# A new order for all engines of a delta-rule and gated-MLP kernel, operations and buffers as before

## The chip, the cores and the metric

One core of a Trainium2 chip runs the whole program. The metric is device time in microseconds, the median of several executions. PE is the matrix engine (TensorE), DVE VectorE, ACT ScalarE, POOL GpSimd, and SP issues the loads and stores. Each engine executes its own list of instructions in order, and waits on semaphores for what the others have to deliver.

## The reference

Four batches of eight heads run a delta rule over 768 time steps with a 48 x 48 state per head; its output, 384 wide, goes through a gated MLP with a mixing over time.

```
k_n = k / (norm(k) + 1e-6)
for t in range(768):
    y[t]  = q[t] @ state
    v_old = k_n[t] @ state
    state = state + beta[t] * outer(k_n[t], v[t] - v_old)
h = relu(x @ w_in);  u, v = h[:, :512], h[:, 512:]
v_n = (v - mean(v)) / sqrt(var(v) + 1e-6)
out = (u * (w_spatial @ v_n + b_spatial)) @ w_out
```

w_in and w_out come as 64-bit floats, all else as 32-bit.

## The kernel before, in words

The recurrence is cut into chunks of 64 time steps. Two batches are worked on at a time, so there are 24 steps s (two rounds of 12); within a round each needs the state of the one before.

**Preparation.** Steps come in six groups g of four. For a group, PE makes the products of the keys (kk blocks, line 492), copies bring them to SBUF (L500, L503), DVE transposes the diagonal parts (L525), a chain of small instructions makes the norms and scales (L533 to L543), and then a triangular inverse is built column by column. Group 0 does it for blocks of 16 (L576 and L581, 15 columns), with ACT's L549 writing the diagonal first, L586 copying the result out, DVE's L595 transposing it back, and two rounds of widening (two PE blocks w16e and w16f, ACT's L683 between them, DVE's L685 and shifts behind them). The other groups do it for blocks of 32: 61 "lane" instructions on DVE (L563 and L568) beside their counterparts on POOL, then L595 and shifts on ACT and POOL (L327, zeros L331 and L333). For each pair of steps L625, PE blocks e and f, ACT's L646 and L651 widen the result to 64.

**A step.** PE blocks kq (masked by DVE's L724), a (subtracted from v by L747), qs, b (copied by ACT's L777), c (added to the state by L792 or L790) and pu; the output goes out by ACT's L807, is put in place by small loads (xs), and is cast and split by L827 and L828. v is scaled before by L707. The loads of step s + 2 take the buffer of step s.

**Weights.** w_in and w_out are made 32-bit by hand (load, L392, L394 to L397, L398, L400 to L403), and all weights are split in a high and a low half for the faster matmuls (L383 on ACT, L384 on DVE or POOL).

**MLP.** Chunks of two or three large matmuls (B512, B256, B384) with their evictions: L851 to L880 for v and its norm, L904 for u, L945, L962 to L968 for the gate, L983 for the output.

All of this is 2642 operations in a plan. `ORDER` lists them in the order in which the program issues them; each engine's own list is what the order leaves for it. A number w in it stands for operation w // 4, and w % 4 chooses among the engines on which that operation may run (DVE or POOL for the subtractions, ACT or POOL for some copies).

```
    words = [int(w) for w in ORDER.split()]
    with tc.manual_schedule():
        P.issue([divmod(w, 4) for w in words])
```

Buffers and PSUM banks are taken from small pools when an operation is issued, in the order of the list, so the list also says which unit each operation gets.

Of the kernel before, what the change touches and what calls it, by code (L numbers as in the profile page):

```python
# [36 lines left out]
28 0 24 52 64 40 928 448 8 32 20 12 56 37 4 68 61 44 936 1076 72 85 80 48  # L37
89 1064 92 97 292 100 344 108 452 112 456 116 1080 120 468 124 128 132 1100 1084 136 140 500 460
76 1068 144 608 464 396 296 148 552 1072 1088 472 152 1692 932 104 348 476 312 504 156 480 164 1696
352 485 168 1104 172 300 176 624 612 180 184 304 489 188 192 628 196 200 356 400 204 616 632 416  # L40
208 696 621 212 492 216 1108 220 160 224 508 1092 228 692 232 664 497 404 236 2384 240 1096 244 2348
248 308 1129 252 2336 256 512 1112 1121 260 264 408 268 1729 272 276 520 556 280 316 412 668 680 284
1125 672 684 677 360 940 944 560 364 708 688 1732 572 368 712 716 948 564 1117 952 1736 516 420 372
320 376 16 324 380 568 720 956 724 524 1004 728 328 968 576 732 988 332 980 740 736 1000 985 960
1008 972 289 744 1012 424 748 528 580 428 752 584 432 994 965 1060 1016 996 976 437 1640 1020 532 1132
1644 1048 1029 1026 1689 1040 1648 756 1652 588 1136 1656 1660 1054 1140 1044 1144 1056 1148 1664 536 1668 1152 1034
1680 1700 1156 1672 1160 1036 1980 2340 1704 1164 1676 1168 592 1708 1189 1684 336 540 760 1724 2344 1712 1172 1180
1740 1176 1184 596 1716 1196 1296 1200 1308 1744 1312 1984 1720 764 1204 341 636 1208 1748 1992 1212 440 1216 1220
1752 1988 1224 2029 1996 1228 1232 1756 385 1236 1760 1240 1244 1248 1768 388 601 1252 1256 1260 1772 1764 1324 1796
2032 1328 1264 1340 1784 392 652 640 2000 2332 444 1788 2040 1268 1344 2008 2036 1792 1356 2004 1360 644 1272 1780  # L50
2020 2048 1372 2044 1800 2016 1376 1276 2052 656 648 1776 2056 1280 700 661 2060 1284 1804 2068 1288 1292 2072 704
1808 872 2012 2352 2076 544 2024 1300 1388 2372 2356 1304 1392 2360 1316 1404 1320 1408 2084 2064 549 1332 2092 1336
892 1348 604 1916 2081 1352 2088 1420 1364 2100 2096 1424 1368 1436 2104 1380 1440 1384 1452 1396 1836 876 2108 1400
1456 880 1192 1412 1468 2112 1416 1472 2120 1428 1432 1484 1920 1444 2124 1488 1448 1924 884 1500 1460 2152 1928 1464
1504 1932 888 1476 2144 1516 2376 1480 1520 1492 2132 896 1936 2380 3796 1496 1532 1508 1940 2364 1536 1512 1944 900
1840 1524 1548 3784 904 1528 1552 1540 1844 2140 2368 1544 1564 1556 1812 1568 2400 2136 1560 1580 1572 1816 1576 1584
2116 2148 1588 1848 909 2396 1592 2128 1852 1856 2961 2392 1948 2388 2964 912 1620 1952 2404 1601 1628 2972 1609 1626
1956 1960 1596 1606 1964 2968 1632 1968 1614 1820 1636 3013 916 1616 2912 1824 2408 2452 1828 920 2916 2156 2412 2976
768 3016 2920 2416 2160 2924 1832 2928 2932 3020 1972 2164 1861 2940 2420 2936 2424 2168 2428 1864 2952 2432 2980 3432
# [1046 lines left out]
```

## Time and profile before

| | us |
|---|---|
| median of 3 runs | 452.54 (451.09 to 455.63) |
| the profiled execution | 450.03 |
| its span, first to last instruction | 448.3 |
| PE busy / DVE / ACT / POOL | 401.3 / 284.8 / 252.6 / 173.9 |

The profiled execution is one of its own, a little faster than the median. Its span leaves out 1.73 us around the program. Durations in the prediction are those of this one execution.

### The profile page before, as it was taken

Reading aid. Unit: us, or ns where it says so; the run is one execution under the profiler, and the core shown is the slowest. Engines: PE = TensorE matmul, PEld = TensorE weight load, DVE = VectorE, ACT = ScalarE, POOL = GpSimd, SP = SyncE. Lnnn points to the kernel's source line nnn. Section 1 sums busy time; section 2 is a strip of 40 time slices with the busy share of each in tenths; the row PEclk is TensorE's granted clock in tenths of the full one; section 3 lists DMA queues with packets and bytes.
Section 4 is the critical chain, followed back from the end, with each engine's and each line's share of the span. In section 5 each row is a group of like instructions: output and inputs, shape, how many; then the busy total and the mean of one; then the engine's idle time right before and its main releaser. Section 6 shows DMA issues by size and latency. Waiting matters only on the chain.

```text
span 448.3 us, 19504 instructions
## 1 busy us (share of the span) xinstructions
PE 401.3 (90%) x8648; PEld 363.5 (81%) x8648; DVE 284.8 (64%) x697; ACT 252.6 (56%) x551; POOL 173.9 (39%) x343
## 2 busy tenths in 40 slices
PE   4325677999899999999999999999999999999996
PEld 3214566778688898778889889899889899999996
DVE  3799899988868876638898988833313324431331
ACT  3898763796677742976466834373426772231112
POOL 5270278628770863313785465612111110110010
PEclk9555586999999999999999999999999999999999
DMA  8941057222542332122351232032300000000102
GB/s 269 350 161 40 4 185 263 95 86 93 194 140 102 117 123 102 41 95 95 108 178 39 85 112 83 5 111 86 111 30 1 2 35 1 1 35 37 54 35 89
DMA packets 16020, 42.51 MB, mean 95 GB/s; under 512 B 3392, under 2 KB 7616, under 8 KB 15936
## 3 DMA queue, kind: packets, MB, share of 16 engines
q1 hardware_dynamic: 15936, 41.27, 27.1%
q8 instruction: 68, 1.11, 1.0%
q14 instruction: 16, 0.13, 0.1%
HBM read 35.36 MB, written 4.72 MB: 89 GB/s over the span
## 4 chain that ended last, share of the span: by engine, by line
PE 76%; DMA 8%; ACT 5%; DVE 5%; SPq 2%; issue 2%; POOL 1%; ACTq 0%; DVEq 0%; POOLq 0%
PE ps L453 76%; DMA bn<-in_bun 3%; SPq L348 2%; DMA ke<-in_k_t 2%; DMA vf<-in_w_in 2%; ACT xt L327 1%; DVE xt L595 1%; DVE ps L581 1%; DVE prod L576 1%; DMA xs<-xs 1%; DMA bn<-in_k_t 1%; ACT xh L827 1%; ACT tn L646 1%; DVE wsp_l L384 0%; DVE pt L724 0%
## 5 line engine op out<-in xcount | busy, mean ns | idle before, releaser
L453 PE MATMUL ps<-wsp_h,vf 128*128 128x256 f32 x480 | 104.3, 286 | 0.0
L453 PEld LDWEIGHTS ps<-wsp_h,vf 128*128 128x128 f32 x480 | 80.8, 188 | 1.4
L453 PE MATMUL ps<-wsp_l,vf 128*128 128x256 f32 x240 | 67.5, 281 | 0.0
L568 DVE TENSOR_TENSOR ps<-ps,prod 128x60 f32<-128x60 f32 (+9 forms) x150 | 46.0, 307 | 4.3
L563 DVE TENSOR_TENSOR prod<-ps,la 128x60 f32<-128x60 f32 (+9 forms) x150 | 44.7, 298 | 4.0
L453 PEld LDWEIGHTS ps<-wsp_l,vf 128*128 128x128 f32 x240 | 45.2, 188 | 0.3
L962 DVE TENSOR_TENSOR gt<-ps,bbc 128x512 f32<-128x512 f32 x18 | 12.4, 692 | 43.6 <-PE ps L453 43.6
L568 POOL TENSOR_TENSOR wl<-wl,prod 128x36 f32<-128x36 f32 (+4 forms) x90 | 31.9, 354 | 6.7
L563 POOL TENSOR_TENSOR prod<-wl,la 128x36 f32<-128x36 f32 (+4 forms) x90 | 31.1, 345 | 5.9
L453 PE MATMUL ps<-ke 64*64 64x64 f32 x704 | 18.2, 253 | 13.8 <-ACT xt L327 5.2
L453 PE MATMUL ps<-wout_h,g 128*128 128x384 f32 x112 | 30.5, 342 | 0.0
L453 PEld LDWEIGHTS ps<-ke 64*64 64x64 f32 x704 | 15.2, 161 | 17.4 <-ACT xt L327 7.0
L983 ACT COPY ob<-ps 128x384 f32<-128x384 f32 x24 | 11.4, 479 | 26.9 <-PE ps L453 23.2
L453 PE MATMUL ps<-bn 64*64 64x64 f32 x832 | 20.1, 241 | 6.6 <-DMA bn<-in_k_t 3.6
L777 ACT COPY w<-ps 128x384 f32<-128x384 f32 x24 | 11.5, 480 | 24.6 <-PE ps L453 24.5
L968 POOL TENSOR_TENSOR xt<-gt,xt 128x512 fp32r<-128x512 f32 x3 | 3.9, 1285 | 55.1 <-ACT xt L967 55.1
L453 PE MATMUL ps<-wsp_h,bn 128*128 128x256 f32 x96 | 24.7, 281 | 0.0
L453 PEld LDWEIGHTS ps<-bn 64*64 64x64 f32 x832 | 16.6, 150 | 9.9 <-issue 3.9
L651 ACT COPY xt<-ps 32x256 f32<-32x256 f32 x48 | 17.4, 363 | 10.2 <-PE ps L453 9.5
L453 PE MATMUL ps<-xh,win_h 128*128 128x256 f32 x120 | 22.5, 296 | 0.8 <-ACT vr L851 0.8
L807 ACT COPY xs<-ps 112x512 f32<-112x512 f32 x22 | 12.9, 585 | 17.4 <-PE ps L453 17.2
L453 PE MATMUL ps<-wout_h,xt 128*128 128x384 f32 x80 | 22.0, 338 | 0.0
(192 smaller groups left out, 1088.8 us busy)
## 6 DMA issues: line engine op xcount, KB each, us to landing
bn<-in_bun SPq DMA_DIRECT2D x22, 896.0 KB, 4.9
ke<-in_k_t SPq DMA_DIRECT2D x22, 256.0 KB, 3.7
out<-ob SPq DMA_DIRECT2D x24, 192.0 KB, 1.9
vf<-in_w_in SPq DMA_DIRECT2D x6, 512.0 KB, 6.9
g<-in_w_sp SPq DMA_DIRECT2D x3, 768.0 KB, 4.4
g<-in_w_out SPq DMA_DIRECT2D x4, 384.0 KB, 3.1
bn<-in_bun SPq DMA_DIRECT2D x2, 640.0 KB, 8.1
xs<-xs SPq DMA_DIRECT2D x66, 16.0 KB, 2.4
```

The costliest lines, as they stand in the source:

```text
L327: (nc.scalar.copy if e == "ACT" else ENG[e].tensor_copy)(out=out_, in_=in_)
L348: return P.add({"SP": 0.55}, lambda: nc.sync.dma_start(out=out_() if callable(out_) else out_, in_=in_() if callable(in_) else in_), rd, w ...
L453: nc.tensor.matmul(o, l, r, start=start, stop=stop)
L563: P.add({eng: cost}, lambda: e.tensor_tensor(out=dst if j == i0 else pt, in0=w[:, :n, j : j + 1].broadcast_to([128, n, m]), in1=la3[:, j, ...
L568: P.add({eng: cost}, lambda: e.tensor_tensor(out=dst, in0=dst, in1=pt, op=ALU.add), rd=[pk], wr=[key], due=due)
L576: P.add({"DVE": cost}, lambda: nc.vector.tensor_tensor(out=dst if j == 0 else pt, in0=w4[:, :, :n, j : j + 1].broadcast_to([128, 2, n, m]) ...
L581: P.add({"DVE": cost}, lambda: nc.vector.tensor_tensor(out=dst, in0=dst, in1=pt, op=ALU.add), rd=[("prod", "DVE")], wr=["wp"], due=due)
L651: P.add({"ACT": 0.46}, lambda r=i(a), f=f: nc.scalar.copy(out=v()[r, :, f, :], in_=pq4[r, :, f - 1, :]), rd=["pe0"], wr=[("fo", s + par, a ...
L777: P.add({"ACT": 0.48}, lambda: nc.scalar.copy(out=v3(w, 192), in_=v3(pc, 512)[:, :, 0:192]), rd=["pc"], wr=[("w", s % 2)], due=due + 2)
L807: nc.scalar.copy(out=x.rearrange("p (s j t) -> p s j t", s=4, j=2)[0:KR, :, :, s % 2 * 64 : s % 2 * 64 + 64], in_=pq.rearrange("p (s c) -> ...
L962: P.add({"DVE": 0.69}, lambda: nc.vector.tensor_tensor(out=gt(), in0=v3(bank(h.unit), 256), in1=v3(sums(p, half), 256) if p else bias(th), ...
L983: P.add({"ACT": 0.48}, lambda: nc.scalar.copy(out=ob_[t.unit], in_=bank(h.unit)[:, :DM]), rd=[("po", b, th, o)], wr=[("ob", b, th, o)], du ...
```

## The change

Only the list changes. Another search wrote it, one that judges an order by draws of noise on the durations that change during the search. The operations, their dependencies and the pools are the same. By engine, the list before has 886 operations on PE, 697 on DVE, 502 on ACT, 321 on POOL and 164 on SP; the new one 886, 691, 496, 333 and 164. 140 operations run on another engine than before (98 between DVE and POOL, 34 between ACT and POOL, 8 between ACT and DVE). Within its engine's list an operation moves by a median of two places on PE, DVE and POOL, four on ACT, one on SP; at most by 60.

```diff
 ORDER = """
-28 0 24 52 64 40 928 448 8 32 20 12 56 37 4 68 61 44 936 1076 72 85 80 48
-89 1064 92 97 292 100 344 108 452 112 456 116 1080 120 468 124 128 132 1100 1084 136 140 500 460
-76 1068 144 608 464 396 296 148 552 1072 1088 472 152 1692 932 104 348 476 312 504 156 480 164 1696
-352 485 168 1104 172 300 176 624 612 180 184 304 489 188 192 628 196 200 356 400 204 616 632 416
+8 0 28 20 12 52 64 40 16 80 4 448 32 24 56 36 68 1064 60 44 936 88 1076 73
+85 292 49 928 96 93 104 100 452 108 1080 152 112 116 456 120 124 1100 1084 128 160 500 132 460
+296 1068 344 136 464 140 608 148 1088 1072 144 552 156 468 1692 1112 164 472 300 396 168 312 1696 932
+172 1104 176 476 180 480 504 184 2348 348 1108 188 485 508 192 612 624 196 352 200 204 1092 628 489
...
 10336 10340
 """
```

The parts of it that the prediction speaks of, by engine (operation number and line):

```
DVE ahead of the first L576, behind the first L543
  before  74 L392, 37 L543, 118 L398, 87 L392, 119 L400, 126 L392, 41 L576
  after   36 L543, 41 L576   (118, 119, 126, 87 stand between the next L576 and L581)
DVE between the last L581 of group 0 and L595
  before  139 L392, 79 L398, 71 L595
  after   432 L707, 71 L595   (432 was on POOL; 158 L384 is on POOL now)
ACT between L586 and the first L683
  before  103 L396, 168 L383, 171 L383, 90 L396, 140 L394, 91 L397, 143 L397
  after   128 L395, 281 L327, 102 L395, 90 L396, 77 L396, 168 L383, 171 L383, 140 L394, 103 L396
SP, the first loads
  before  7, 13, 16, 10 keys, 232 step 0, 112 w_in, 269 keys, 20 beta, 266 keys, 73, 86 w_in, 275 keys, 125 w_in, 152 w_sp, 99, 138 w_in
  after   7, 13, 16, 10 keys, 20 beta, 112 w_in, 266, 269 keys, 73 w_in, 232 step 0, 275 keys, 125, 86 w_in, 152 w_sp, 272 keys, 138 w_in
DVE behind the first lane of group 1 (299 L563)
  before  300 L563, 436 L747, 191 L384, 301 L568
  after   83 L403, 300 L563, 301 L568, 191 L384, 96 L403, 302 L563, 436 L747
PE, steps 0 to 2
  before  425 b, 585 kk, 427 c, 435 a, 429 pu, 496 e, 437 qs, 438 b, 440 c, 442 pu, 508 kq, 500 f, 510 a
  after   425 b, 427 c, 585 kk, 435 a, 429 pu, 496 e, 437 qs, 438 b, 442 pu, 440 c, 500 f, 508 kq, 510 a
```

## Rows read from the trace of the kernel before

**Rows 1.** The page: busy time of each engine with its share of the span, and the granted clock of PE in 40 slices of 11.2 us, in tenths of full speed.

```profile
PE 401.3 (90%) x8648; PEld 363.5 (81%) x8648; DVE 284.8 (64%) x697; ACT 252.6 (56%) x551; POOL 173.9 (39%) x343
...
PEclk9555586999999999999999999999999999999999
```

**Rows 2.** Busy time by stretch (from and to in us, then the length; x is the number of instructions; then the clock as a share of full speed, the DMA share and GB/s).

```profile
0.00:20.00 20.00, 7.15 (x226) 6.21 (x227) 10.19 (x24) 11.35 (x20) 8.42 (x31) 0.79 0.88 297
20.00:45.00 25.00, 9.38 (x558) 8.31 (x561) 23.55 (x57) 22.73 (x40) 10.21 (x12) 0.50 0.37 130
...
60.00:93.42 33.42, 26.76 (x707) 21.83 (x699) 30.95 (x78) 20.90 (x41) 25.77 (x47) 0.85 0.50 170
93.42:200.00 106.58, 102.69 (x2795) 87.96 (x2795) 79.90 (x224) 73.72 (x176) 51.52 (x118) 1.00 0.33 109
200.00:448.30 248.30, 244.13 (x3957) 228.93 (x3947) 127.25 (x290) 112.83 (x249) 73.23 (x129) 1.00 0.18 60
```

The five busy times in each row are PE, its weight loads, DVE, ACT and POOL.

**Rows 3.** The chain of work that ended last, in order of time: start, length, what.

```profile
11.97 6.82 DMA vf<-in_w_in
...
42.37 0.39 ACT ob L683
...
327.59 117.20 PE ps L453 x899
444.86 0.48 ACT ob L983
```

**Rows 4.** DVE in order of time, up to L595 of group 0: start, length, line, operation, out<-in, shapes; in brackets the idle time before it and what ended that.

```profile
13.57 0.27 DVE L506 MEMSET ps<- 128x256 f32 x1
...
18.81 0.43 DVE L392 TENSOR_SCALAR ut<-vf 128x512 uint32<-128x512 uint32 x1 [2.17 <-DMA vf<-in_w_in]
...
22.85 0.95 DVE L384 TENSOR_TENSOR wsp_l<-g,wsp_h 128x768 fp32r<-128x768 f32 x1
...
28.92 0.85 DVE L392 TENSOR_SCALAR ut<-vf 128x512 uint32<-128x512 uint32 x1
29.70 0.68 DVE L398 SCALAR_TENSOR_TENSOR ut<-vf,ut 128x512 uint32<-128x512 uint32 x1
30.30 2.07 DVE L595 STREAM_TRANSPOSE xt<-wl 128x1024 f32<-128x1024 f32 x1
```

**Rows 5.** ACT in order of time, around the first L683.

```profile
29.05 0.59 ACT L586 COPY wl<-ps 128x512 f32<-128x512 f32 x1 [0.44 <-DVE ps L581]
...
30.16 1.55 ACT L383 CAST wsp_h<-g 128x768 fp32r<-128x768 f32 x2
...
33.98 0.37 ACT L683 ACTIVATE ob<-ps 128x256 f32<-128x256 f32 x1
```

**Rows 6.** PE in order of time: the first block w16e, and the first matmuls of block e of steps 0 and 1 and of steps 4 and 5.

```profile
32.42 1.26 PE L453 MATMUL ps<-xt,bbc 32*16 32x16 f32 x128 [6.85 <-DVE xt L595]
...
47.05 0.63 PE L453 MATMUL ps<-tn,xt 32*32 32x32 f32 x27 [1.15 <-DVE tn L625]
...
93.42 0.75 PE L453 MATMUL ps<-tn,xt 32*32 32x32 f32 x64
```

**Rows 7.** Busy time by stretch, as in rows 2: from the end of L586 to L683; from L525 of group 1 to its first lane; the lanes, up to L595; from L595 to L625.

```profile
29.64:33.98 4.34, 1.56 (x140) 1.52 (x144) 4.31 (x5) 4.34 (x8) 2.80 (x3) 0.50 0.26 92
...
46.91:57.10 10.19, 7.45 (x236) 6.82 (x240) 8.96 (x20) 7.97 (x21) 1.56 (x3) 0.50 0.10 18
57.10:86.68 29.58, 23.77 (x765) 20.08 (x758) 27.83 (x78) 16.66 (x33) 24.00 (x46) 0.79 0.52 182
...
86.68:92.65 5.97, 5.19 (x88) 4.23 (x88) 5.13 (x5) 5.62 (x11) 3.27 (x6) 1.00 0.53 184
```

**Rows 8.** DVE in order of time, beside the lanes of group 1 and after them.

```profile
57.94 1.51 DVE L384 TENSOR_TENSOR wout_l<-g,wout_h 128x384 fp32r<-128x384 f32 x1
...
65.21 1.28 DVE L384 TENSOR_TENSOR win_l<-ut,win_h 128x512 fp32r<-128x512 f32 x2
...
68.38 2.05 DVE L384 TENSOR_TENSOR wsp_l<-g,wsp_h 128x768 fp32r<-128x768 f32 x1
...
85.97 0.54 DVE L790 TENSOR_TENSOR s<-s,ps 112x384 f32<-112x384 f32 x1
...
93.28 0.52 DVE L384 TENSOR_TENSOR wout_l<-g,wout_h 128x384 fp32r<-128x384 f32 x1
...
94.53 0.96 DVE L828 TENSOR_TENSOR xl<-xs,xh 128x768 fp32r<-128x768 f32 x1
```

**Rows 9.** POOL in order of time, two of the same splits.

```profile
57.76 1.27 POOL L384 TENSOR_TENSOR win_l<-ut,win_h 128x512 fp32r<-128x512 f32 x1
...
67.81 1.81 POOL L384 TENSOR_TENSOR wsp_l<-g,wsp_h 128x768 fp32r<-128x768 f32 x1 [0.28 <-ACT wsp_h L383]
```

**Rows 10.** Groups of instructions by line, engine and shape: busy time, mean ns of one, idle time before them and what ended it.

```profile
L965 DVE TENSOR_TENSOR gt<-gt,ut 128x512 f32<-128x512 f32 x15 | 10.8, 720 | 0.5
...
L707 DVE TENSOR_TENSOR bn<-bn,nn 128x384 f32<-128x384 f32 x7 | 4.3, 611 | 1.9 <-DMA bn<-in_bun 1.9
...
L403 DVE TENSOR_TENSOR ut<-ut 128x512 f32<-128x512 f32 x3 | 2.0, 685 | 0.0
...
L965 POOL TENSOR_TENSOR gt<-gt,ut 128x512 f32<-128x512 f32 x9 | 12.1, 1341 | 12.9 <-DVE gt L962 6.5 <-DVE st L868 6.2
```

212 rows, old and new, of the table ORDER are left out of this document.

## The prediction, made before the change was run

> **What bounds the kernel now.** I read the shares and slices of the page first. PE is busy 90% of the span, and the granted clock stands at half in slices 2 to 5, comes back in slice 6 and dips once more in slice 7 (67 to 78 us) before it stays [rows 1]. So there are two stages with different limits, and the table of stretches puts numbers on them [rows 2]. In the first 45 us PE works 16.5 us and DVE 33.7 us, of which 23.55 in the 25 us from 20 to 45. From 60 to 93.42 DVE is still the fuller one (30.95 of 33.42 us, PE 26.76). From 93.42 to 200 PE is busy 102.69 of 106.58 us, from 200 to the end 244.13 of 248.30. 93.42 is where PE starts block e of steps 4 and 5 [rows 6], the first PE work that needs group 1 of the preparation.
>
> The reading for this change: the PE list is a fixed heap of matmuls. Before and after, exactly the same 66 PE operations stand ahead of that block e, and 820 from it on, so an order can only win by bringing that point forward, or by closing PE gaps behind it. The gaps behind it are 3.89 + 4.17 us [rows 2], and 3.5 us of the latter are the last copy and store, from 444.8 [rows 3] to 448.3, which no order removes: 4.6 us are on offer there. What sets 93.42 is the chain of group 0, in the chain view a file of DVE and ACT instructions from the first loads on [rows 3], and then the 61 lane instructions of group 1 on DVE.
>
> **The change, part by part.** I wrote the two lists out by engine, and took every duration from the trace of before. The profiled execution took 450.03 us: 448.3 of span and 1.73 around it. The median of the runs shown is 452.54, so I work against 450.03 and carry the difference over to 452.54. About 1% of that, 4.5 us, is the least that a measurement of this kernel can tell from no change.
>
> *The wait for a weight load goes.* In the old list DVE has L392 of op 126 ahead of the first L576. It waits 2.17 us for a w_in load that was issued at 11.97 and lands at 18.79 [rows 3, 4], with nothing to do meanwhile. The new list has the first L576 straight after the two L543, and puts the L392s between later lane instructions. There, adding up the durations, op 126 comes at about 18.5, and its load is issued with 0.5 MB less ahead of it, so I cost that edit's new wait at nothing; should the load be as late as before, it is 0.3 us. L549, on which the first L576 also depends, moves ahead of two L397 on ACT. DVE also has less work ahead of L595: L506 (0.27), one L384 (0.95), one L392 (0.85) and one L398 (0.68) go behind it or to POOL [rows 4], one L707 (0.61 [rows 10]) comes from POOL: -2.1 us. L595 moves from 30.30 by 2.2 (the wait alone) to 4.3 us (both in full). Some of it is lost to L549 and to the copy L586 (0.59 [rows 5]), so I take -3.5.
>
> *ACT takes most of that back.* L595 releases block w16e on PE, and its result is copied by L683 on ACT. Between L586 and L683 ACT has 7 instructions in the old list and has no gap (4.34 us busy of 4.34 [rows 7]); in the new list it has 9. Two more, at 4.34 us for 7, are +1.2; and two of the nine are the casts of the second w_sp load, which is issued once the first is split, on POOL as far as I can see at about the old time: they stood at 30.16 [rows 5] and are 6th and 7th in line now, so that they can hardly come much earlier, and L683, which follows two instructions behind them, lands at some 32.4. It was already at ACT's pace: its input ended at 33.68 [rows 6], it began at 33.98 [rows 5]. So it comes 1.6 us earlier and not 3.5; by ACT's two instructions alone it would be 2.3. Now w16f, L685, the shifts, again w16e and w16f and L625 follow. DVE has 1.3 us more between L595 and L685, hidden by PE's w16f; ACT 0.5 less up to its first shift; from there to L625 the DVE work is the same within 0.1 us. So block e of steps 0 and 1 (47.05 [rows 6]) and L525 of group 1 (46.91) come some 1.4 us earlier.
>
> *From L525 to the lanes of group 1.* DVE has 8.96 us busy in these 10.19 us [rows 7]; the new list puts 0.6 us more there (one L402 and one L403 in, one L403 and one memset out), which its 1.23 us of idle may or may not cover, since one part of that idle is the wait for PE's block c of step 0. The start of the lanes moves by -1.4 to -0.2; I take -0.8.
>
> *The lanes.* From 57.10 to 86.68 DVE executes 78 instructions with 27.83 us busy of 29.58 [rows 7]: this is the bound, and work in or out counts whole. Out go an L384 of w_sp (2.05), an L384 of w_in (half of the 1.28 for two) and an L790 (0.54), in come two L403 (0.69 each) and one L384 of w_in (0.64) [rows 8, 10]: -1.2 us. But the 2.05 us ran beside POOL's L384 of the same size (1.81 at 67.81 [rows 9]); L828, a subtraction of the same size and types, takes 0.96 alone [rows 8], and by that the sum is -0.1. I take the middle, -0.6. POOL gets one L384 of w_sp and one of w_in there and gives up one of w_in and one L403, some 0.7 us more; it has 5.6 us of idle in this stretch [rows 7], so its own lanes stay hidden.
>
> A split on DVE is stretched by one on POOL: L384 of w_out takes 1.51 us at 57.94, after POOL's L384 began at 57.76, and 0.52 us at 93.28 [rows 8, 9]. The Trainium skill, page "SBUF — State Buffer", section "Who interferes with whom", has a rule for that: a DVE instruction with two SBUF inputs and a GpSimd instruction that reads SBUF block each other in full. By the rule each of the three instructions that come to DVE would also meet a POOL lane, and the sum for the lanes would be above zero; by the rows of DVE alone it is -0.6.
>
> *From L595 to block e of steps 4 and 5.* One L384 (0.52), the L790 (0.54 [rows 8]) and one L747 come between L595 and L625, an L403 and an L724 go: one instruction more, +0.4, against 0.84 us of idle in that stretch [rows 7]. I take +0.3.
>
> *Sum up to block e:* -0.8 - 0.6 + 0.3 = -1.1 us, between -2.6 and +0.1.
>
> *Behind block e.* All PE blocks and chunks are there in both lists, moved by a median of two places. The trace cannot show what the gaps of another interleaving are. From below, the 4.6 us on offer go entirely; from above, I let as much be added. I take 0, nearest to the fact that the number of changes between small and large matmuls is about the same (80 and 83 in the two lists), as is the cover: for links of one instruction between two PE blocks (L646, L777, L747, L503, L724, L807 and so on) I counted the PE work that the list puts between both blocks against the duration of the link, and what is short sums to 14.3 us in the old list and to 14.0 in the new. Other parts (swaps of DVE and POOL in the gate's L965 and L968, order of loads, the last operations of the list) stand under full PE slices and cost nothing; if that cover fails, a swap costs 0.6 us, the difference of L965 on the two engines [rows 10].
>
> So 450.03 - 1.1 = 448.9 against the profiled execution, and 452.54 - 1.1 = **451.4** against the median.
>
> **The rivals.**
> *A, the early gain is kept.* If ACT executes its nine instructions sooner than I think (the w_sp load landing early), all of L595's 3.5 us reaches block e. For it: the chain view has L683 only in its second round [rows 3]. Against it: ACT without a gap. Time 449.0, still inside 1%.
> *B, faster: the PE gaps close as well.* A search that judges orders by disturbed durations might leave more room between the links. Sum -1.1 - 4.6 = -5.7, time 446.8. For it: 8 us of gaps, most of them ahead of 200 us. Against it: the cover counted above is the same.
> *C, slower: step 1 is held up on DVE.* L747 of step 1 has five more instructions ahead of it (L403 twice, L384 and two short lane instructions: 0.69 + 0.69 + 1.51 is 2.9 us, and the lanes some more [rows 8, 10]). Behind it stand block b of step 1, its state and its outputs, and all of steps 2 and 3, which PE has in line ahead of block e. The clock came back to full in slice 6 and was at half again in slice 7 [rows 1]; a PE that waits at 59 may keep the half clock for longer. Three us of delay and two more of slower matmuls: +5.0, time 457.5. It decides as soon as steps 1 to 3 end later than group 1; today PE has 6.7 us of idle between 60 and 93.42 to soak it up [rows 2], which speaks against it.
> *D, nothing comes of it.* The three DVE instructions that join the lanes each wait for POOL, whose lanes run all the time there. Some 0.4 us each eats the -1.1, and the L384 of w_out was stretched by 0.99 [rows 8]: 452.5. Against it: the new list takes the 2.05 us split out of just this situation. It is also what the rule of the Trainium skill's page "SBUF — State Buffer" would make of this change.
>
> **How the numbers follow.** Forecast 0.40, A 0.15, B 0.20, C 0.13, D 0.12. The likeliest is 451.4. The range takes in the bounds of the sum, 452.54 - 2.6 - 4.6 = 445.3 and 452.54 + 0.1 + 4.6 = 457.2; leaving out the outer tails of B and C, 446 to 457. Faster by over 1% (below 448.0): B in most cases and the edge of A and the forecast, 0.22. Slower by over 1% (above 457.1): most of C and the edge of D, 0.15. Within 1%: 0.63.
>
> **What would show it.** In the profile of the changed kernel: no idle time of DVE for a w_in load ahead of the first L576, and L595 at about 26.8; L683 at about 32.4, directly behind another ACT instruction; block e of steps 0 and 1 at about 45.7; the lanes of group 1 from about 56.3 and L595 of group 1 at about 85.3; block e of steps 4 and 5 at about 92.3; from there to the end of the span 355 us, as now. If L683 comes before 31.5, A was right; if from block e to the end it is under 352, B; if block b of step 1 starts after 61 and PE's clock is at half in 60 to 70, C. Wrong altogether I would be if the loads ran in another manner: the first 20 us move 297 GB/s [rows 2], and a later load of step 0 or 1 would hold PE up where I have no row for it.

## The result, and the profile after

The new list took 457.06 us (median of 20 runs, 454.79 to 460.84), the old one beside it 452.63 (449.50 to 456.08). The ratio is 1.0103 (95% interval 1.008 to 1.0125), so the change makes the kernel 1% slower. The profiled execution took 457.71, with a span of 455.8.

The page after has the same work in it; PE is busy 401.5 us, where [rows 1] has 401.3:

```profile
PE 401.5 (88%) x8648; PEld 363.4 (80%) x8648; DVE 278.1 (61%) x691; ACT 251.1 (55%) x545; POOL 180.2 (40%) x355
...
PEclk9555595989999999999999999999999999999999
```

The table of stretches of the new kernel, cut at its own block e of steps 4 and 5 (97.03), answers to [rows 2]:

```profile
0.00:20.00 20.00, 8.32 (x256) 7.33 (x256) 11.30 (x28) 11.81 (x21) 6.56 (x30) 0.77 0.82 269
20.00:45.00 25.00, 7.11 (x468) 6.37 (x472) 21.43 (x48) 20.91 (x36) 10.30 (x12) 0.50 0.41 152
60.00:97.03 37.03, 27.92 (x764) 23.57 (x758) 30.76 (x80) 22.81 (x44) 27.72 (x51) 0.82 0.52 171
97.03:200.00 102.97, 97.22 (x2563) 83.24 (x2562) 75.88 (x218) 67.60 (x161) 53.13 (x116) 1.00 0.30 101
200.00:455.80 255.80, 250.49 (x4179) 233.36 (x4177) 125.06 (x288) 116.96 (x259) 79.44 (x141) 1.00 0.18 62
```

Block e comes 3.61 us later than in [rows 6], and behind it PE's idle time is 5.75 + 5.31 us where it was 3.89 + 4.17. So this one execution loses half ahead of the block and half behind it. The experiments show that the first half is not the list's.

The early waits can be read engine by engine. ACT of the new kernel, from the copy of the keys (a helper's line) to the first L683:

```profile
24.67 0.58 ACT L327 COPY xt<-ps 128x512 f32<-128x512 f32 x1 [0.47 <-PE ps L453]
...
29.53 0.56 ACT L586 COPY wl<-ps 128x512 f32<-128x512 f32 x1
...
32.98 1.55 ACT L383 CAST wsp_h<-g 128x768 fp32r<-128x768 f32 x2
...
35.67 0.36 ACT L683 ACTIVATE ob<-ps 128x256 f32<-128x256 f32 x1
```

DVE of the new kernel:

```profile
15.93 0.20 DVE L576 TENSOR_TENSOR ps<-ps,la 128x30 f32<-128x30 f32 x1
...
26.57 1.59 DVE L392 TENSOR_SCALAR ut<-vf 128x512 uint32<-128x512 uint32 x1
...
28.55 0.20 DVE L581 TENSOR_TENSOR ps<-ps,prod 128x30 f32<-128x30 f32 x1
...
30.12 2.10 DVE L595 STREAM_TRANSPOSE xt<-wl 128x1024 f32<-128x1024 f32 x1 [0.86 <-ACT wl L586]
...
89.05 2.12 DVE L595 STREAM_TRANSPOSE xt<-wl 128x1024 f32<-128x1024 f32 x1 [1.55 <-POOL wl L568]
91.08 0.50 DVE L790 TENSOR_TENSOR s<-s,ps 112x384 f32<-112x384 f32 x1
```

In the kernel before, the first L576 stood here:

```profile
19.15 0.19 DVE L576 TENSOR_TENSOR ps<-ps,la 128x30 f32<-128x30 f32 x1
```

The first L576 comes at 15.93, 3.2 us earlier than before, and nothing of it is left at L595: 30.12 against 30.30 [rows 4]. L595 waits 0.86 us for ACT's L586, and DVE itself is done with the 15 columns only at 28.75: of the L392s that now stand among them one takes 1.59 us and one, at 19.23, 1.36, where the one at 18.81 took 0.43 in the kernel before [rows 4]. Both run beside a POOL instruction, the first of them beside this one:

```profile
26.06 1.82 POOL L384 TENSOR_TENSOR wsp_l<-g,wsp_h 128x768 fp32r<-128x768 f32 x1 [0.60 <-ACT wsp_h L383]
```

At L595 of group 1 DVE waits 1.55 us for POOL, whose lanes stand behind an L707 that waits for a load:

```profile
75.80 0.83 POOL L707 TENSOR_TENSOR bn<-bn,nn 128x384 f32<-128x384 f32 x1 [4.80 <-DMA bl<-in_b_l]
...
88.78 0.24 POOL L568 TENSOR_TENSOR wl<-wl,prod 128x19 f32<-128x19 f32 x1
```

The L790 that stands behind that L595 holds PE's block a of step 4, and with it all that PE has in line:

```profile
91.64 0.68 PE L453 MATMUL ps<-s,bn 64*64 64x48 f32 x32 [1.79 <-DVE s L790]
...
93.78 0.84 PE L453 MATMUL ps<-xl,win_h 128*128 128x256 f32 x3
...
96.58 0.52 PE L453 MATMUL ps<-xl,win_h 128*128 128x256 f32 x3
97.03 0.75 PE L453 MATMUL ps<-tn,xt 32*32 32x32 f32 x64
```

Behind that wait three matmuls of 256 columns take 0.84 us, and 0.52 from 96 on: PE works at half clock for a while (in the row of this stretch the granted clock is the 0.50 behind the five busy times). In the profile of before it didn't there.

```profile
92.68:96.10 3.42, 3.42 (x13) 2.93 (x12) 3.00 (x5) 1.56 (x3) 2.98 (x5) 0.50 0.47 152
```

Behind block e, where the granted clock is 1.00 in both kernels, PE's waits by what it waited for (us in total, times, longest), first in the new kernel, then in the old one:

```profile
PE ps L453 <- DMA ke<-in_k_t: 2.2, 2, 1.4
PE ps L453 <- DMA bn<-in_bun: 1.3, 1, 1.3
PE ps L453 <- ACT xs L807: 0.9, 2, 0.5
PE ps L453 <- ACT w L777: 0.6, 1, 0.6
...
```

```profile
PE ps L453 <- ACT tn L646: 1.0, 2, 0.6
PE ps L453 <- DMA bn<-in_bun: 0.9, 1, 0.9
PE ps L453 <- DMA ke<-in_k_t: 0.7, 1, 0.7
...
```

All waits of over 0.15 us behind block e sum to 7.3 us in the new kernel and to 4.2 in the old one. The longest of the new ones, 1.42 us, is that of kk block 953 for key load 952 (953, 952 and the like are operation numbers), which goes into the buffer that kk block 947 has just freed.

### The profile page after: what moved, and what is told of

Same layout as the page of the kernel before. It is cut to its first block, busy times and chain, and to the rows that moved or that the text cites. A ratio compares the mean times of both kernels' runs of the same rounds, so it can differ in the third digit from the quotient of the medians.

```text
span 455.8 us, 19527 instructions
## 1 busy us (share of the span) xinstructions
PE 401.5 (88%) x8648; PEld 363.4 (80%) x8648; DVE 278.1 (61%) x691; ACT 251.1 (55%) x545; POOL 180.2 (40%) x355
## 3 DMA queue, kind: packets, MB, share of 16 engines
q8 instruction: 68, 1.11, 1.0%
## 4 chain that ended last, share of the span: by engine, by line
PE 71%; DMA 9%; ACT 7%; DVE 6%; SPq 3%; issue 2%; POOL 1%; DVEq 0%; ACTq 0%; POOLq 0%
PE ps L453 71%; DMA ke<-in_k_t 5%; SPq L348 3%; DMA g<-in_w_out 2%; DVE xt L595 1%; DMA xs<-xs 1%; DMA bn<-in_bun 1%; ACT xt L327 1%; ACT xs L807 1%; DVE la L525 1%; ACT xh L827 1%; ACT win_h L383 1%; ACT xt L331 1%; ACT xt L651 0%; ACT w L777 0%
## 5 line engine op out<-in xcount | busy, mean ns | idle before, releaser
L453 PE MATMUL ps<-wsp_h,vf 128*128 128x256 f32 x480 | 103.2, 287 | 0.0
L568 POOL TENSOR_TENSOR wl<-wl,prod 128x36 f32<-128x36 f32 (+4 forms) x90 | 30.9, 343 | 6.4
L968 POOL TENSOR_TENSOR g<-gt,g 128x512 fp32r<-128x512 f32 x9 | 11.5, 1286 | 37.3 <-ACT g L967 37.3
L327 POOL COPY xt<-xt 32x512 f32<-32x512 f32 (+1 forms) x24 | 13.8, 575 | 30.3 <-DVE xt L685 13.0
L967 ACT CAST xt<-gt 128x512 fp32r<-128x512 f32 x10 | 6.2, 621 | 33.6 <-DVE gt L965 20.8
L453 PE MATMUL ps<-wsp_h,bn 128*128 128x256 f32 x96 | 23.3, 281 | 0.0
```

The source lines that it names most:

```text
L327: (nc.scalar.copy if e == "ACT" else ENG[e].tensor_copy)(out=out_, in_=in_)
L453: nc.tensor.matmul(o, l, r, start=start, stop=stop)
L568: P.add({eng: cost}, lambda: e.tensor_tensor(out=dst, in0=dst, in1=pt, op=ALU.add), rd=[pk], wr=[key], due=due)
L967: P.add({"ACT": 0.62}, lambda: nc.scalar.copy(out=gv(gg)[0][:, hs], in_=gt_[t.unit]), rd=[kk], wr=[("gh", b, th, half)], due=due + 6)
L968: P.add(both(512), lambda e: ENG[e].tensor_sub(out=gv(gg)[1][:, hs], in0=gt_[t.unit], in1=gv(gg)[0][:, hs]), rd=[kk, ("gh", b, th, half)], ...
```

## The experiments

Two numbers stand for each: the ratio to the old list with its 95% interval, and the time from the start of PE's block e of steps 4 and 5 to the end of its last matmul in the profiled execution, called "behind block e" (before: 93.42 to 444.79, 351.4 us; after: 355.3). The first is a median of several executions, the second comes from one. All are lists of the same 2642 operations. What a list has up to block e is its start, what it has from there its rest.

**Which half of the list?** The two hybrids:

```diff
 # h1_old_start
+old list up to block e of steps 4 and 5 (operation 729)
 new order and engines for all others
 # h2_new_start
+new list up to operation 729
 old order and engines for all others
```

> The old list up to PE's block e of steps 4 and 5 (operation 729), and from there the remaining operations in the new list's order with its engine choices. Theory S (the whole loss is made in the start, before that block; what follows only passes it on): the time of before, 452.6, and the block at 93.4. Theory L (the new list's order behind the block costs by itself, through key and v loads that are issued later): 457, with the block at 93.4 and more idle time of PE behind it than the 8 us of before. As the profiled executions split it (3.6 us in place by the block, 3.9 behind it): 454.8.

> The mirror image: the new list up to operation 729, then the old order and its engine choices. Theory S: the time of after, 457, with the block at about 97. Theory L: 452.6 plus whatever the old order can't hide of a late start, at most 2 us. As the profiled executions split it: 454.8. If both hybrids sit at 457, neither part is at fault by itself and the two halves of a list depend on each other.

The old start with the new rest took 459.3 us (1.0142, 1.0108 to 1.0176; 356.0 behind block e), the new start with the old rest 451.36 (0.997, 0.9949 to 0.9991; 352.0). Theory S falls and theory L holds for where the loss is made; that late loads make it, as L had it, these two don't show. The first hybrid also shows what the profiled start is worth. Up to block e its list is the old one, and it is late too:

```profile
32.70 0.59 ACT L586 COPY wl<-ps 128x512 f32<-128x512 f32 x1 [2.61 <-DVE ps L581]
```

L586 stood at 29.05 in the profile of before [rows 5], and block e comes at 95.84 here against 93.42. One list, two executions, 2.4 us apart at block e, with DVE waiting for w_in loads in both. The new start, unchanged, stands in thirteen of the executions profiled here, under different rests: block e comes between 91.84 and 97.03 in them, at 94.59 on average, and the profile after is the latest of all. Block e of steps 0 and 1 comes between 45.53 and 48.08, and from there to block e of steps 4 and 5 it takes 46.1 to 49.0 us. Behind block e the old rest repeats within 0.9 us in five executions (351.1 to 352.0).

**Engines or places?**

```diff
 # e_old_order_new_engines
 old order
+the engine of the new list for each of the 140 operations
```

> Every operation stands in the old list's place, but the 140 operations that changed their engine run on the new one. Theory of places (a chain of late starts by the order: ACT behind a late key load, L707 on POOL ahead of lanes, L790 behind L595): 452.6, within 1 us, with the block e of steps 4 and 5 at 93.4 to 94.5. Theory of engines (what was moved to POOL, 12 operations more, is slower there and sets the end of the lanes): 455 to 457 and POOL's lanes of group 1 ending after DVE's.

453.6 us (1.0012, 0.9985 to 1.004), behind block e 353.6; block e at 94.82. The time is at the edge of what the theory of places allows, and far from that of engines.

```diff
 # r_old_engines
 new order
+behind operation 729 the engine of the old list for 109 operations
```

> The new list, but behind block e of steps 4 and 5 the 109 operations that changed their engine run on the one they had before. The old order with the new engines took 353.6 us behind block e, 2.2 more than before, and its time was 0.5 us over before's, not separable from nothing. Theory of engines (half of the loss behind block e is the choice of engine): 353 to 353.5 behind block e, time 455. Theory of order: 355 to 356, time 456.5 to 457.5.

457.62 us (1.0119, 1.0092 to 1.0147), behind block e 358.4. Timed, the places carry the loss: the old order with the new engines can't be told from before, and the new order with the old engines is as slow as the new list (1.0119 against 1.0103). In the traces, one execution each, the new engines alone cost 2.2 us behind block e, the new places alone 7.1, both together 3.9. That the engines fit the order with which they were found is what this suggests; the timed runs don't show it.

**The two waits at the end of the start.**

```diff
 # e_both: the new list, and
 # POOL
-520 L707 of step 3, 137 L384, lanes 347, 348, 351, 352
+lanes 347, 348, 351, 352, 520 L707 of step 3, 137 L384
 # DVE
-398 L595 of group 1, 529 L790 of step 3
+529 L790 of step 3, 398 L595 of group 1
```

> The new list with two places of it mended: the four POOL lane instructions that stand behind POOL's L707 of step 3 (which waits 4.80 us for a load) stand ahead of it, as in the old list, and the L790 of step 3 stands ahead of DVE's L595 of group 1. My theory: DVE's L595 no longer waits 1.55 us for POOL and starts at about 88 less the L790's 0.54, PE's block a of step 4 no longer waits 1.79 us for L790, so the block e of steps 4 and 5 starts at 94.5 to 95.5 in place of 97.03, and the time is 455 to 455.8, 1.2 to 2 us under the new list's. Rival (the start is not what counts; key loads behind it are): the block comes earlier, and the time stays at 457.

456.64 us (1.0086, 1.0055 to 1.0117), behind block e 355.9. DVE no longer waits for POOL at L595 and PE no longer for L790, but L790 itself now waits 1.04 us for PE, and block e, now held by L625, comes at 95.34. That is where the theory had it, but also inside the range of the start without these edits; the time stays, as the rival had it. The same two edits on the hybrid with the old rest:

> The list of the hybrid with the new start (451.36) and in that start the two mended places: POOL's four lane instructions ahead of POOL's L707 of step 3, and L790 of step 3 ahead of DVE's L595 of group 1. With the new rest the two were worth 0.4 us, not separable from nothing, where I had expected 1.2 to 2. Theory (L595 and block e of steps 4 and 5 come earlier and the old rest keeps it): 450.5, and DVE's L595 of group 1 without a wait for POOL. Rival (steps 2 and 3 or group 1's L625 end at the same time by other waits, nothing is gained): 451.4.

452.15 us (0.9999, 0.9973 to 1.0025; 351.1). The rival holds: no gain that can be measured.

**ACT's order in the start.**

```diff
 # s_act_early: h2_new_start, and
 # ACT
-91, 130 L397, 279 L523, 123 L383, 101 L394, 70 L586
+70 L586, 91, 130 L397, 279 L523, 123 L383, 101 L394
-168, 171 L383, 140 L394, 103 L396, 237 L683
+237 L683, 168, 171 L383, 140 L394, 103 L396
 # DVE
-66 L576, 100 L392, 67 to 69 L581, L576, L581, 432 L707, 71 L595
+66 L576, 67 to 69 L581, L576, L581, 100 L392, 432 L707, 71 L595
-169 L384, 79 L398
+79 L398, 169 L384
```

> The hybrid with the new start and the old rest (451.36), with the start's list changed on ACT and DVE alone: the copy L586 of group 0 stands ahead of seven ACT instructions (L397 twice, L523, L383, L394 and the L395 pair around them) and the DVE lanes that it needs ahead of one L392; the first L683 stands ahead of the two casts of the second w_sp load; one L398 changes places with the L384 that needs them. This is my prediction's first step put to the test: L595 was to come 3.5 us earlier and came 0.2 earlier, because ACT's L586 stood behind the copy of key load 272, which waits for that load, and seven more instructions. Theory (ACT's order alone takes the 3.5 us): L595 at 27.5 to 28.5, L683 at 32 to 33, and as DVE is busy from there to L595 of group 1, that comes 1 to 2 us earlier too: 449.5 to 450.5. Rival (it is not ACT: the loads of w_sp and keys set L683 and the lanes): L595 comes earlier, the lanes of group 1 start at 58.5 as before, and the time stays at 451.4.

452.08 us (1.0023, 0.9999 to 1.0046; 351.3). My theory that ACT alone took the 3.5 us falls. L586 has moved up (by five instructions, not seven as I wrote), and now waits for DVE:

```profile
28.55 0.59 ACT L586 COPY wl<-ps 128x512 f32<-128x512 f32 x1 [1.07 <-DVE ps L581]
```

On DVE the 15 columns end only at 28.52, and an L707 stands in the way, stretched from 0.61 to 1.19 us:

```profile
28.32 0.20 DVE L581 TENSOR_TENSOR ps<-ps,prod 128x30 f32<-128x30 f32 x1
...
28.95 1.19 DVE L707 TENSOR_TENSOR bn<-bn,nn 128x384 f32<-128x384 f32 x1
30.05 2.02 DVE L595 STREAM_TRANSPOSE xt<-wl 128x1024 f32<-128x1024 f32 x1
```

L683, now ahead of the two w_sp casts, still came only at 35.04.

**Once more the new start with the old rest**, to see whether its 0.997 was the list's:

> The hybrid of the new start with the old rest once more, unchanged. It is the only list with a time under before's whose interval kept clear of 1 (0.997, 0.9949 to 0.9991); two lists with the same rest and small changes in the start gave 0.9999 and 1.0023. If the start is worth the 1.1 us that I forecast for it: 0.996 to 0.998 again. If the first result was a lucky draw of early loads: 0.999 to 1.002, and the start is worth nothing that can be measured.

451.99 us (0.9996, 0.9971 to 1.0021; 351.4). With the two lists above (c_h2_both and s_act_early), the new start on the old rest has 0.997, 0.9999, 1.0023 and 0.9996: nothing that can be told from no change. None of these is a version that beats the old kernel.

**Where in the rest?** First two cuts:

```diff
 # m_new_to_200:   new list up to block a of step 12 (operation 1697), then the old order
 # m_new_from_200: new to 729, old to 1697, then the new order
```

> The new list up to PE's block a of step 12 (operation 1697, at about 200 us), the old order from there. The two hybrids put the start of the new list at -1.2 us against before and its rest behind block e of steps 4 and 5 at +5.7 to +6.8. Theory of the middle (the loss is made between 97 and 200 us, where preparation, steps and MLP chunks are interleaved and where after's rows show PE waiting for the key load 952 and the bun load): 456 to 457. Theory of the end (it is made behind 200 us): 451 to 452. Going by the starting times of PE's operations in the profiled executions, some 3 us lie ahead of 200 and under 1 us behind: 454.5.

> The mirror image: the new list up to operation 729, the old order from there to operation 1697, the new order behind it. Theory of the middle: 451 to 452. Theory of the end: 456 to 457. Going by the starting times in the profiled executions: 452 to 453.

456.5 us (1.0087, 1.0059 to 1.0116; 358.6) and 454.15 (1.004, 1.0013 to 1.0067; 353.4). Most lies ahead of 200 us, but not all. In the traces the two together exceed the loss of the whole (7.2 and 2.0 us for 3.9); timed, 0.87% and 0.40% for 1.03% are within the intervals. Four smaller grafts, cut where both lists have nearly the same operations behind them:

```diff
 # h2_new_start with one stretch in the new order and on its engines:
 # g_729_880 (95 to 115 us), g_880_1113 (115 to 141), g_1113_1302 (141 to 223), g_1302_end
```

> The hybrid with the new start and the old rest (451.36; 352.0 us from block e of steps 4 and 5 to PE's last matmul), in which only the 171 operations from that block to block pu of step 6 (operation 880, about 95 to 115 us) stand in the new list's order with its engines. By the starting times of PE's blocks the new rest has lost 1.0 us against the old one there. Theory (the losses are local: each stretch's order carries its own, and the four grafts sum to the 3.3 to 4 us): 353.0 behind block e, time 452.4. Rival (the new order is only slow as one whole, or a graft costs by its seams): the four sum to something else.

> The same, with only the 189 operations from block pu of step 6 to operation 1113 (about 115 to 141 us: steps 7 and 8, the key loads 949 to 955, block e of steps 8 and 9) in the new order. In the new rest PE waits there 1.4 us for key load 952 and 0.4 longer for the bun load, and has lost 1.0 to 1.2 us more by the end of it. Local theory: 353.0 to 353.2 behind block e, time 452.5. If key loads are the cause after all, the wait of kk 953 shows here; if it is handed on, the stretch behind 141 us is as in the old rest and the loss stays.

> The same, with only the 567 operations from operation 1113 to MLP chunk 1302 (about 141 to 223 us) in the new order. The new rest has lost some 0.6 us more at the end of it. Local theory: 352.6 behind block e, time 452.

> The same, with only the last 1186 operations, from MLP chunk 1302 on (from about 223 us), in the new order. The new rest has lost 0.7 us more there, with PE waiting 0.76 us for key load 1851. Local theory: 352.7 behind block e, time 452.1.

| graft | us | ratio (95%) | behind block e | over the old rest's 351.4 |
|---|---|---|---|---|
| 95 to 115 | 452.86 | 0.9997 (0.9971 to 1.0023) | 352.8 | 1.4 |
| 115 to 141 | 453.94 | 1.0021 (0.9994 to 1.0048) | 354.9 | 3.5 |
| 141 to 223 | 454.13 | 1.0032 (1.0005 to 1.0059) | 352.8 | 1.4 |
| 223 to end | 451.73 | 0.9985 (0.9961 to 1.0009) | 351.8 | 0.4 |

In the traces the loss is local: each graft adds, within 0.5 us, what the new list loses in the same stretch (by PE's start times 0.9, 1.7, 1.0 and 0.3), except for the second, which adds 1.8 more. There PE waits for key load 952 and its clock then goes down. PE around that wait, and the stretches around it (the figure behind the five busy times is the granted clock):

```profile
117.89 0.69 PE L453 MATMUL ps<-ke 64*64 64x64 f32 x32 [0.98 <-ACT xs L807]
...
132.32 0.69 PE L453 MATMUL ps<-ke 64*64 64x64 f32 x32 [1.61 <-DMA ke<-in_k_t]
```

```profile
130.00:134.00 4.00, 2.39 (x74) 1.96 (x73) 1.78 (x3) 2.56 (x6) 2.41 (x6) 1.00 0.24 80
134.00:138.00 4.00, 4.00 (x55) 3.78 (x47) 0.71 (x1) 2.52 (x6) 1.20 (x3) 0.57 0.68 232
138.00:142.00 4.00, 3.40 (x148) 3.15 (x139) 3.50 (x4) 3.07 (x11) 2.72 (x3) 1.00 0.03 10
```

PE is at half clock for 3.4 us, from 134.1 to 137.5, and busy all the while: some 1.7 us are lost by that, about the 1.8 that the graft has over. The list that is new up to 200 us has the same dip (0.57 from 134.8 to 138.8) behind the same wait. The new list itself has the wait (1.42 us, up to 135.74) without the dip, so the dip is no part of its 3.9 us:

```profile
134.00:138.00 4.00, 2.58 (x75) 2.15 (x74) 1.38 (x3) 2.75 (x6) 2.78 (x5) 1.00 0.18 65
138.00:142.00 4.00, 3.41 (x147) 3.09 (x147) 2.57 (x4) 3.44 (x9) 2.49 (x3) 1.00 0.68 236
```

Timed, only the third graft is clear of 1. The four sum to 0.35% over 1, that is 0.0047 over the 0.9997 at which their common base lies on average; the whole new rest has about 0.012. The intervals of the four ratios combine to about 0.005 either way, so this doesn't settle whether the sum falls short.

**Is it the key loads?** On the new list:

```diff
 # e_keys_covered: the new list, and
 # ORDER: 952 key load directly behind 947 kk; SP's own list stays 958, 901, 952
 # PE
-805 chunk, 953 kk, 808 to 813 chunks, 1103 kq
+805, 808 to 813 chunks, 953 kk, 1103 kq
-1745 chunk, 1852 kk, 1320, 1746, 1321 chunks
+1745, 1320, 1746, 1321 chunks, 1852 kk
```

> The new list with two places behind block e mended: the key load 952 stands right behind the kk block 947 whose buffer it takes (two other transfers stood between), and the kk block 953 that needs it stands five PE chunk matmuls later; the kk block 1852, which waits for key load 1851, stands three matmuls later. Theory (waits of PE for keys that are loaded into a buffer just freed are the loss): the waits of 1.42 us at 135.7 and 0.76 us at 241 go, 2.2 us in all, 454.9. Rival (the PE work put into the gap is missing elsewhere, or the next link, L525 of that group or block kq of step 8, then waits): the key waits go and the time stays within 0.7 us of 457.

457.79 us (1.0118, 1.007 to 1.0165; 355.1): the rival, if 0.1 us outside the band it was given. The expectation is wrong on one point: the key load was not moved. The transfers that stand between 947 and 952 on SP, 958 and 901, come ahead of 947 in `ORDER` already, so SP's list is the same, and 952 is issued 1.27 us behind the start of kk 947, for 1.38 in the new list. What the run tests is the later place of kk 953 and kk 1852 (the copy of kk 953's result on ACT moves with it). Both key waits are gone, and PE behind block e waits for others instead, 6.7 us in all for 7.3:

```profile
PE ps L453 <- ACT xt L327: 1.7, 3, 0.7
PE ps L453 <- ACT xs L807: 1.6, 2, 1.1
PE ps L453 <- DVE tn L625: 0.7, 2, 0.4
...
```

**Many waits at once** (eight blocks of the new list, where the expectation says ten; six of the old rest, with one chunk for both a 1697 and b 1700):

```diff
 # e_fill: the new list, with one or two chunk matmuls pulled ahead of
+kk 1852, kk 1855, c 1702, e 1673, kk 1532, kq 1204, kq 884; four ahead of kk 953
 # (952 behind 947 in ORDER only, as above)
 # c_best: s_act_early, with one chunk matmul pulled ahead of
+kk 1852, b 1700, a 1697, e 1673, b 889, kq 884
```

> The new list with ten of its PE waits behind block e of steps 4 and 5 filled together: ahead of each block that waits 0.4 to 1.5 us in the profile after (kk 953, kk 1852, kk 1855, c 1702, e 1673, kk 1532, kq 1204, kq 884) the next one or two chunk matmuls are pulled forward, kk 953 stands behind four of them, and key load 952 directly behind kk 947. From block e to PE's last matmul the old rest takes 351.1 to 352.0 us in the profiled executions, the new rest 355.1 to 356.0, with the two key waits mended or not. Theory (the loss is many links from one PE block to the next that have too little PE work put between; mending one hands the wait to the next link of the same step, mending them together gives it back): 352 to 353.5 behind block e, time 454 to 455.5. Rival (the later links are set by DVE and ACT, which run late as a whole in the new order): the waits move on and the stretch stays over 354.5, time 456.5 to 457.5.

> The list of the run with L586 early, with six of the PE waits behind block e filled as in the filled new list (kk 1852, b 1700, a 1697, e 1673, b 889, kq 884, one chunk matmul each). If filling pays on the old rest as well: 350 to 351 us behind block e and 0.5 to 1.5 us under the run with L586 early alone. If a chunk matmul pulled forward only delays what stands behind it: the same time within 0.5 us.

457.21 us (1.0119, 1.0094 to 1.0144; 356.2) and 453.88 (1.0054, 1.0029 to 1.0079; 353.2). The first is the rival's result, though not shown to be so by its mechanism: of the 356.2 us, 1.58 are a stop of PE of another kind, which comes up below. The second is worse than either side had it. It adds 1.9 us to the old rest's 351.3; that a chunk matmul pulled forward delays what stands behind it is the likely reading. Timed, the two intervals (1.0029 to 1.0079, and 0.9999 to 1.0046 without the six) still overlap.

**The key load in its own stretch**, on the graft that carries most in the traces:

```diff
 # g_880_keys: g_880_1113, and 953 behind four chunk matmuls more
 # (952 directly behind 947 in ORDER only, as above)
```

> The graft of the stretch from 115 to 141 us (354.9 us from block e to PE's last matmul, where the old rest takes 351.1 to 352.0), with key load 952 directly behind kk 947 and kk 953 four chunk matmuls later, two of them left between it and block kq of step 8. If the key load is this stretch's own cause, the wait of 1.68 us goes and 353.0 to 353.5 remain behind block e. If it only stood in for the link behind it, 354.5 to 355, with a new wait between 131 and 140 us. Timed: 452.9 against 453.9, at the edge of what five rounds tell.

454.52 us (1.0041, 1.002 to 1.0063; 354.4). The wait of 1.6 us is gone and the loss stays, as the rival had it, with a new wait between 131 and 140 us. But up to block kq of step 8, where the same PE work is done in all these lists, this execution has made the loss good: kq starts 39.9 us behind block e, for 43.1 in the graft and 39.8 before. It is lost again behind that, and by what was not in my list. PE's instructions there, and the stretch from 138 on, with the granted clock at 0.59:

```profile
135.16 0.75 PE L453 MATMUL ps<-tn,xt 32*32 32x32 f32 x64 [0.48 <-DVE tn L625]
136.19 0.45 PE L453 MATMUL ps<-s,bn 64*64 64x48 f32 x16 [0.28 <-DVE s L790]
137.94 0.68 PE L453 MATMUL ps<-s,bn 64*64 64x48 f32 x16 [1.30 <-issue]
```

```profile
138.00:142.00 4.00, 4.00 (x61) 3.75 (x61) 1.07 (x3) 1.53 (x5) 0.88 (x2) 0.59 0.02 4
```

Block a of step 8 stops in its middle, for nothing that the profile can name. With the 3.4 us at half clock behind it (some 1.7 us lost) the stop is most of what the run has over, so it doesn't tell what the mended wait alone is worth. The filled list stops behind the same matmul, the 3154th of PE's list, for 1.58 us. The records of the DMA queue that brings PE's instructions, in packets of 16 KB, go with it (us; in 17 of the 20 profiled executions one packet starts when PE has reached its 6059th to 6073rd instruction, matmuls and weight loads counted; "PE there" is the 6061st):

```
              PE there   packet starts   it ends   PE goes on
before          131.56          131.66    132.64   no stop
after           137.75          138.56    139.51   no stop
g_880_1113      134.54          134.67    135.60   no stop
g_880_keys      132.84          135.68    136.66   137.94
e_fill          133.51          136.64    137.59   138.88
e_keys_covered  134.29          135.75    136.63   no stop
```

The other three of the 20 are the lists with the later kk 953. In two of them the packet starts some 3 us late, and PE goes on 1.3 us after it has landed; in the third it is 1.5 us late, and PE doesn't stop. In these three the 896 KB bun load, which takes the buffer that block c of step 7 frees, is issued 1.5 to 2.1 us before PE is at that place, as c no longer stands behind the wait of kk 953; in the other 17 it is 0.2 to 0.6 us. In the graft with kk 953 moved:

```profile
131.31 0.33 SPq L348 DMA_DIRECT2D bn<-in_bun  x1
```

In all three the packet starts 0.4 to 1.0 us before this load has landed. That it is this load that holds the packet up is what the times suggest; it was not tested by moving the load.

## Why the prediction was wrong

*Behind block e: the step that failed.* I took 0 between -4.6 and +4.6, on the ground that as many changes between small and large matmuls and as much cover stood in both lists. The runs show +3.9 in the profiled execution and +4.6 with the old start; six lists with the new rest lie between 1.0086 and 1.0142, four runs of the old rest with the new start between 0.997 and 1.0023, so about 1.2%, 5 us, is the rest's. PE's visible waits there are 7.3 us, for 4.2. My count of cover had links from one PE block to the next through an engine. It left out the loads into a buffer just freed (952 and 1851 behind the kk blocks 947 and 1846, 2.9 and 3.9 us from issue to landing). They are 2.2 us of the waits, but covering them moved no time, so which links make the loss is not shown. The bound was wide enough for the size in the traces. What was wrong was to take its middle, and to let the sum of cover speak for places.

*Up to block e: the size holds, the steps don't.* I had -1.1 us, between -2.6 and +0.1. The new start on the old rest averages 0.9997, -0.1 us, with intervals of about 1 us to either side. Within it: the w_in wait ahead of the first L576 went as said (15.93 for 19.15). L595 didn't come at 26.8, but at 30.12. I had left out that ACT's L586 stands behind the copy of a key block, which waits for its load, and I had booked the L392s among the columns at the length that they had before, where two took 1.36 and 1.59 us beside POOL; with L586 moved up it was DVE that held L595. The chain of the new kernel has that load with 9.05 us:

```profile
14.29 9.05 DMA ke<-in_k_t
```

L683 was announced at 32.4 and came at 35.67; the w_sp casts ahead of it came at 32.98 and not at about 30, but with L683 ahead of them it came at 35.04, so it is ACT's whole list there that sets it. The lanes started at 58.39, not 56.3; "POOL's own lanes stay hidden" was wrong by 1.55 us; and L790, which I booked as a gain for the lanes, held PE for 1.79 us. None of this counted in the end: mending L790 and POOL, or ACT, moved no time. The same start differs from one execution to the next by up to 5.2 us, more than the 1.1 that I forecast for the list. The loads of the first 20 us (0.82 to 0.88 of all DMA engines in both profiles) are one likely reason, which no run tested; about half of the spread is made behind 47 us.

*A 450.03 for a 452.54.* I worked against a profiled execution that was 2.5 us faster than the median, and took the difference along as if it lay nowhere. Most of it lay in the start: 93.42 for block e, where the same list had 95.84 in another execution. Of the 7.68 us between the two profiled executions, 3.6 lie ahead of block e, where the timed runs show no difference.

*The rivals.* A and B fell. C had the right sign and time (457.5), by luck, for it had them in the wrong place: b of step 1 came at 61.41, as C announced, but it came at 62.06 with the old start too, and PE's clock was full from 58.6 to 68.8 and at half up to 79.0, as before (69.6 to 79.8); the start cost nothing. What C had right is the coupling: a wait of PE and then a lower clock, which shows at 92.7 us in the new list and at 134 in the graft, not at 60, and not behind every such wait. D, DVE beside POOL in the lanes: the two L403 that join them took 0.67 and 0.74 us, for 0.69 [rows 10], and the L384s of w_in 0.81 and 0.68, for 0.64 [rows 8], so some 0.2 us for the three that D had at 0.4 each; the L384 of w_out took 0.55, for 1.51, as POOL wasn't splitting beside it. The rule that D named, of the Trainium skill's page "SBUF — State Buffer", section "Who interferes with whom", agrees with the 0.81, which began 0.06 us behind a POOL lane, and decided nothing in the lanes.

*What stays open.* The traces give the new rest 3.7 to 4.8 us in the five lists with the new engines, the timed runs some 5. Which places in the order make it is open: every wait that was covered was followed by others. And whether the sum of the four stretches is the whole, the timing can't say.

## What to carry to other kernels

Before a difference between two profiles is explained, see how far two executions of one list differ in that stretch: here up to 5.2 us in the first 97 us, and 0.9 us in the 351 us behind them. A hybrid of two lists, cut where both have done the same work, told what reading every wait had not. A wait that was covered here was handed on to other links, so the price of this order was that of a stretch, not of any one visible wait. And an edit of an issue order should be read again in each engine's own list: moving an operation between those of other engines moves nothing.

## What the runs showed of the hardware

- PE can run out of instructions. Its 17296 instructions come in 68 packets of 16 KB (1.11 MB in the page's queue q8); two executions show a stop of 1.30 and 1.58 us behind the same matmul when a packet started some 3 us late. The Trainium skill, page "Runtime: NRT & Kernel Launch", section "Instruction fetch mechanics", has the refill in blocks of 16 KiB and calls it mostly hidden. The traces agree on the size, and show where it isn't hidden.
- In the graft from 115 to 141 us, PE was busy 2.39 of the 4 us from 130 to 134, with a wait of 1.61 us, and the granted clock of the next 4 us was 0.57, that is 3.4 us at half (the lower of the two levels), though it had been full from 80 us on. Behind the pause of 1.30 us it was 0.59 from 138 to 142. In the new list PE was busy 2.58 of the 4 us from 134 to 138, with a wait of 1.42 us, and the clock stayed full.
- A key load of 256 KB took 9.05 us from 14.29 on (the DMA engines were busy 0.82 of the first 20 us) and 2.94 from 132.67 on (0.40 of the time from 130 to 134).
- DVE's L392 on 128 x 512 took 0.43 us where it began just ahead of a POOL instruction (18.81 against 18.82, in the kernel before), and 1.59 where it began 0.5 us behind one (26.57 against 26.06, in the new one).
